# Two leading batches, a one-instruction first tile and row gathers on one queue, in the last stage of a linear-attention and spectral-mixing kernel

## The chip, the cores and the metric

The kernel runs on one NeuronCore of one Trainium2 chip. The metric is the device time of one execution in microseconds (us). Executions scatter by about 0.4 us (standard deviation).

## The reference, cut to what matters

```python
def _attn_ref(q, k, v):                      # batch 8, heads 8, sequence 576, head size 64
    q_p, k_p = phi(q), phi(k)                # phi(x) = elu(x) + 1
    kv = einsum('bhsd,bhse->bhde', k_p, v)
    return einsum('bhsd,bhde->bhse', q_p, kv) / (q_p . sum(k_p) + 1e-6)

def _moe_ref(x, w_r, w_i, w_ch):             # x: 8 x 576 x 512
    X = rfft(x, axis=1)                      # only the first 64 modes are kept
    Y = X[:, :64] times (w_r + i w_i), one 512 x 512 complex matrix per mode
    u = x + irfft(Y)
    return u + maximum(u @ w_ch, 0)
```

The weights are 2 x 64 matrices of 512 x 512 in float32, 134 MB in all. The output is 9.44 MB of float32.

## The kernel before

The output has 36 tiles of 128 rows by 512 columns, stored in 18 pairs (16 pairs of `x_main`, two of `x_tail`). A tile needs all 64 modes, so no output tile can be finished before the last mode's weights have arrived. The kernel prepares all it can ahead of that: modes 0 to 31 are folded into `x` and into `E = x @ w_ch` early; modes 32 to 55 are brought into the form `YZ[b]` (one tile for each batch: Y, and Z = Y @ w_ch) during modes 56 to 60. The last eight modes of all batches lie in one tile, `last`, and small DMAs ("gathers", 32 KB each) copy each batch's 16 rows out of it into the free rows 48 to 63 and 112 to 127 of `YZ[b]`. After that, each tile of the tail takes an identity matmul that brings in E, one for Z, a ReLU on ScalarE in place, one for Y, and an add of `x` on VectorE; a pair is then stored.

Batch 0 was a "leading" batch: modes 32 to 55 were applied to its tiles ahead of time, and in the tail it reads `last` directly, through a matrix `inv0_sb` that picks its rows, without waiting for a gather.

```python
for i, dst in enumerate((inv2_sb, inv0_sb)): ...        # row-picking matrices
...
def fold_first(t):                                      # batch 0's four tiles, in modes 56 to 60
    acc = inv2_sb[0:2*NF, rows].T @ YZ[0][0:2*NF, 0, :]  # one matmul
    x = acc + x                                         # VectorE
...
# the end, after the last mode (cut)
for h in range(2): last[:, 1, cols] = YT_rows.T @ wch   # 8 matmuls, two copies
y_ps = transposes of YT_rows                            # 4 transposes
nc.scalar.copy(out=last[:, 0, :], in_=y_ps)
for b in (1, 2, 3, 4, 5, 6, 7, 0):
    eng = nc.sync if b in (1, 2) else nc.gpsimd
    for h in range(2):
        eng.dma_start(out=YZ[b][64*h+48 : 64*h+64, :, :], in_=last[b::B, :, :])
...
rectified(0); rectified(1); channels(2); finish(0)      # rectified: matmuls of Z, then ReLU
channels(3); finish(1); rectified(2); rectified(3)      # channels: matmuls of E
finish(2)                                               # finish: matmuls of Y, add of x, store
for n in range(4, len(pairs)):
    channels(n); rectified(n); finish(n - 1)
finish(len(pairs) - 1)
```

`FILL` adds dummy matmuls in modes 61 to 63 (5, 11 and 6 of them), which keep TensorE busy.

## Time and profile before

The median is 430.0 us (three runs, 429.66 to 430.55); the profiled execution spans 428.4 us.

| part of the span | read from | value |
|---|---|---|
| weight stream, to the last mode's cast | timeline, VectorE | to 394.61 us |
| last mode to `last` complete | timeline, VectorE and ScalarE | to 396.79 us |
| first output store issued | timeline, SyncE | 399.34 us |
| VectorE's last add ends | timeline | 420.90 us |
| stores end (last 0.1 us above 100 GB/s) | windows | 425.5 us |

The last row is read from the windows view in stretches of 0.1 us (its columns are explained below; the last one is GB/s). This is the last stretch above 100 GB/s; the next has 82:

```profile
425.41:425.51 0.10, 0.00 (x0) 0.00 (x0) 0.00 (x0) 0.00 (x0) 0.00 (x0) 0.50 0.41 143
```

The page of the kernel before, part 2: two rows of the span in 40 slices of 10.7 us. The first is the busy share of the 16 DMA engines in tenths, the second what they wrote.

```profile
DMA  8999999999999999999999999999999999995697
GB/s 149 207 208 209 209 210 208 211 215 213 217 213 213 214 213 214 215 212 213 213 213 213 214 214 213 214 213 212 213 214 214 213 214 213 212 214 115 239 405 288
```

For 36 slices the DMA engines are full with the weight stream (the count is of bytes written, as bf16; the float32 bytes read are twice as many). Then comes a slice of 115 GB/s in which the stream drains and nothing can be stored yet, then a slice of 239 that ramps up, and then stores at 405 GB/s. Part 4 of the same page, the chain of work that ended last, by engine:

```profile
DMA 78%; PE 6%; DVE 6%; issue 5%; POOL 2%; ACT 1%; DVEq 0%; POOLq 0%
```

The timeline of VectorE (DVE) in the tail: start, busy time, engine, line, operation, output and inputs, and in brackets the idle time before it and who ended it.

```profile
394.61 0.23 DVE L402 CAST YT<-y_last 128x64 f16<-128x64 f32 x1 [3.11 <-PE y_last L391]
395.98 0.42 DVE L765 CAST last<-zl 128x256 f16<-128x256 f32 x1 [1.14 <-PE zl L757]
398.20 1.29 DVE L684 TENSOR_TENSOR x_main<-acc,x_main 128x512 f32<-128x512 f32 x2 [1.79 <-PE acc L610]
399.42 1.22 DVE L689 TENSOR_TENSOR x_main<-acc,x_main 128x1024 f32<-128x1024 f32 x1
401.34 4.76 DVE L689 TENSOR_TENSOR x_main<-acc,x_main 128x1024 f32<-128x1024 f32 x4 [0.69 <-PE acc L610]
406.37 1.23 DVE L689 TENSOR_TENSOR x_main<-acc,x_main 128x1024 f32<-128x1024 f32 x1 [0.27 <-PE acc L610]
...
419.62 1.28 DVE L684 TENSOR_TENSOR x_main<-acc,x_main 128x512 f32<-128x512 f32 x2
```

VectorE waits 1.79 us for the first tile, 0.69 us for pair 2 and 0.27 us for a gather; then it adds pair after pair. The Trainium skill, "VectorE: DVE Perf Modes", section "The TRN2 errata — SBUF-src ops pay a fixed extra latency per instruction", gives (N+151)/0.96 ns for a float32 tensor add of N columns; that is 691 ns for 512 and, as an estimate from the formula, 1,224 ns for 1,024. This trace agrees, with one of the two inputs in PSUM: the earlier float32 adds of 512 columns have a mean of 691 ns, the pair adds of 1,024 columns 1,223 ns.

The timeline of SyncE's queue, four gathers and then the first stores:

```profile
396.81 2.48 SPq L772 DMA_DIRECT2D YZ<-last  x4
399.34 8.62 SPq L665 DMA_DIRECT2D out_dram<-x_main  x8
```

The first tile's add ended at 398.9 us, but its store was issued only at 399.34, when SyncE had got through its gathers. Last, the windows view, in stretches of 1 us. The last two columns are the share of the 16 DMA engines in use and their GB/s; before them come the stretch's length, the engines' busy times with counts, and the granted TensorE clock.

```profile
397.61:398.61 1.00, 1.00 (x6) 0.49 (x5) 0.41 (x1) 1.00 (x3) 1.00 (x3) 1.00 0.22 66
398.61:399.61 1.00, 1.00 (x5) 0.23 (x3) 1.00 (x3) 0.34 (x1) 1.00 (x3) 1.00 0.47 135
399.61:400.61 1.00, 0.87 (x5) 0.25 (x4) 1.00 (x1) 0.81 (x2) 1.00 (x3) 1.00 0.38 109
400.61:401.61 1.00, 0.88 (x4) 0.11 (x2) 0.31 (x2) 1.00 (x3) 1.00 (x3) 1.00 0.90 305
401.61:402.61 1.00, 1.00 (x8) 0.26 (x6) 1.00 (x2) 0.65 (x2) 1.00 (x3) 1.00 0.92 291
402.61:403.61 1.00, 1.00 (x6) 0.15 (x4) 1.00 (x1) 0.98 (x3) 0.22 (x1) 1.00 1.06 410
```

If one adds up 1 minus the share (taking a share above 1 as 1), the DMA engines left 0.78 + 0.53 + 0.62 + 0.10 + 0.08 = 2.11 us unused here. In the next 1 us they are at 0.88, and from 404.6 us on at 1.00 or above until the stores end.

### The profile page before, as it was taken

What the parts mean: (1) busy time and instruction counts of PE and PEld (TensorE: products, weight loads), DVE (VectorE), ACT (ScalarE), POOL (GpSimd) and SP (SyncE); (2) the same over time, 40 slices, a digit from 0 to 9 for tenths busy, and PEclk for the clock granted to TensorE, in tenths of its full rate; (3) what the DMA queues carried; (4) which work ended last, traced back from release to release, by engine and by line L of the source; (5) the groups of instructions that cost most, each with busy time, mean ns of one, the idle gap of its engine ahead of it and who ended that gap; (6) DMA issues with size and microseconds to landing.
All of it is one profiled execution on the core that took longest, in us unless ns stands there. A gap on an engine that the chain in (4) does not pass through costs nothing.

```text
span 428.4 us, 6567 instructions
## 1 busy us (share of the span) xinstructions
PE 275.9 (64%) x2674; PEld 157.4 (37%) x2674; DVE 208.6 (49%) x426; ACT 149.2 (35%) x231; POOL 94.5 (22%) x171
## 2 busy tenths in 40 slices
PE   0358678786019665655333777787777776988991
PEld 0346556663004433333111334433434433654320
DVE  0699998956003755556100434433443344221792
ACT  3587766631102100000000244443444342220881
POOL 4233223112201321122122121221221221110500
PEclk9999865667558755555555599988999999699996
DMA  8999999999999999999999999999999999995697
GB/s 149 207 208 209 209 210 208 211 215 213 217 213 213 214 213 214 215 212 213 213 213 213 214 214 213 214 213 212 213 214 214 213 214 213 212 214 115 239 405 288
DMA packets 35917, 92.52 MB, mean 216 GB/s; under 512 B 3248, under 2 KB 16432, under 8 KB 35888
## 3 DMA queue, kind: packets, MB, share of 16 engines
q0 software_dynamic: 32192, 82.20, 98.7%
q1 hardware_dynamic: 3696, 9.91, 6.0%
q8 instruction: 21, 0.34, 0.3%
q14 instruction: 8, 0.07, 0.0%
HBM read 163.93 MB, written 9.44 MB: 405 GB/s over the span
## 4 chain that ended last, share of the span: by engine, by line
DMA 78%; PE 6%; DVE 6%; issue 5%; POOL 2%; ACT 1%; DVEq 0%; POOLq 0%
DMA wi<-in_moe_w_i_dram 61%; DMA wr<-in_moe_w_r_dram 5%; DMA pick_sb<-row_pick 4%; DMA q<-in_q_dram 4%; DMA k<-in_k_dram 4%; PE P L349 2%; DVE x L267 2%; PE acc L610 2%; PE acc L649 1%; POOL YZ L772 1%; DMA YZ<-last 1%; DVE qe L195 1%; ACT ke L182 1%; DVE q L189 1%; DVE rd L264 0%
## 5 line engine op out<-in xcount | busy, mean ns | idle before, releaser
L349 PE MATMUL P<-wi,xt_c 128*32 128x512 bf16 x252 | 36.5, 518 | 45.3 <-DMA wi<-in_moe_w_i_dram 45.3
L360 ACT CAST ys<-P 128x512 f16<-128x512 f32 x31 | 18.2, 586 | 134.5 <-PE P L349 134.5
L110 POOL DMA_DIRECT2D wr<-in_moe_w_r_dram x64 | 34.1, 532 | 125.2 <-PE P L349 100.7
L349 PEld LDWEIGHTS <-xt_c 128*32 128x32 bf16 x504 | 30.0, 153 | 83.7 <-issue 72.6
L110 POOL DMA_DIRECT2D wi<-in_moe_w_i_dram x65 | 34.6, 532 | 115.0 <-PE P L349 87.1
L358 DVE CAST ys<-P 128x512 f16<-128x512 f32 x32 | 22.1, 691 | 76.0 <-PE P L349 76.0
L349 PE MATMUL P<-wr,xt_c 128*32 128x512 bf16 x252 | 36.8, 523 | 26.1 <-DMA wr<-in_moe_w_r_dram 24.0
L535 DVE TENSOR_TENSOR x_main<-ya,x_main 128x512 f32<-128x512 f32 x32 | 22.1, 691 | 42.5 <-PE ya L531 42.5
L554 PE MATMUL eps<-wch,xTw 128*128 128x512 f16 x144 | 39.6, 401 | 0.0
L146 PEld LDWEIGHTS <-qT 64*128 64x128 f16 (+1 forms) x640 | 23.5, 125 | 39.6 <-issue 18.9
L365 PE MATMUL yt<-pick_sb,ys 128*128 128x16 f16 x252 | 16.4, 175 | 26.4 <-DMA pick_sb<-row_pick 15.8
L537 ACT CAST x16w<-x_main 128x512 f16<-128x512 f32 x32 | 19.8, 618 | 36.3 <-DVE x_main L535 36.3
L562 ACT CAST E<-eps 128x512 f16<-128x512 f32 (+1 forms) x40 | 21.3, 543 | 24.8 <-PE eps L554 24.8
L146 PE MATMUL num<-kv,qT 64*128 64x65 f16 (+1 forms) x320 | 13.4, 223 | 21.6 <-ACT kv L242 18.8
L365 PEld LDWEIGHTS <-ys 128*128 128x128 f16 x252 | 12.1, 102 | 41.3 <-issue 18.5
L182 ACT ACTIVATE qe<-q 128x1152 f16<-128x1152 f16 x16 | 17.7, 1156 | 22.1 <-DMA q<-in_q_dram 22.1
L211 PE MATMUL qTp<-id,qe 128*128 128x128 f16 x144 | 16.7, 311 | 12.5 <-DVE qe L195 12.1
L267 DVE TENSOR_TENSOR x<-num,rd 128x512 f16<-128x512 f32 x32 | 22.1, 692 | 1.1
L146 PE MATMUL nw<-kv,qT 64*128 64x65 f16 (+1 forms) x320 | 20.0, 235 | 1.4 <-DVE x_tail L506 1.0
L659 ACT ACTIVATE acc<-acc 128x512 f32<-128x512 f32 x36 | 19.1, 581 | 3.2 <-PE acc L610 0.9
L211 PEld LDWEIGHTS <-qe 128*128 128x128 f16 x144 | 14.7, 147 | 13.4 <-DVE qe L195 12.1
L182 ACT ACTIVATE ke<-k 128x1152 f16<-128x1152 f16 x16 | 17.7, 1155 | 4.9 <-DMA k<-in_k_dram 4.9
(90 smaller groups left out, 427.3 us busy)
## 6 DMA issues: line engine op xcount, KB each, us to landing
wr<-in_moe_w_r_dram POOLq DMA_DIRECT2D x64, 512.0 KB, 18.8
wi<-in_moe_w_i_dram POOLq DMA_DIRECT2D x63, 512.0 KB, 18.8
out_dram<-x_main SPq DMA_DIRECT2D x14, 512.0 KB, 4.6
q<-in_q_dram POOLq DMA_DIRECT2D x8, 576.0 KB, 13.4
k<-in_k_dram POOLq DMA_DIRECT2D x8, 576.0 KB, 14.8
v<-in_v_dram POOLq DMA_DIRECT2D x8, 576.0 KB, 16.9
out_dram<-x_main SPq DMA_DIRECT2D x4, 256.0 KB, 4.2
out_dram<-x_tail SPq DMA_DIRECT2D x2, 512.0 KB, 5.3
```

Of the source, the lines that this page charges most:

```text
L110: tc.keep_in_program_order(nc.gpsimd.dma_start(out=w[:, dcs], in_=rows_of[:, dcs, :]))
L146: mm = nc.tensor.matmul(num[hpo][orow, c0 : c0 + 65], qT[rows, hpp, h2, cols], kv_sb[rows, hpp, h2, :])
L182: pin(nc.scalar.activation(out=ev[:, c], in_=heads(nm, b)[:, c], func=AF.Exp))
L211: nc.tensor.transpose(qT_ps[:, j].rearrange("p t r -> p (t r)"), phi["q", b][:, hpp, j].rearrange("p o d -> p (o d)"), id16,)
L267: nc.vector.tensor_tensor(out=dst.rearrange("p (o c d) -> p o c d", o=2, c=4), in0=nv[:, :, :, 0:64], in1=rden.unsqueeze(3).broadcast_to([ ...
L349: nc.tensor.matmul(P[dc * 32 : dc * 32 + 32, :], xt_cols(dc, t, kk), w[:, dc, :], start=(t == 1), stop=(t == 0), tile_position=(0, dc * 32),)
L358: fixed(nc.vector.tensor_copy(out=st, in_=P))
L365: nc.tensor.matmul(yt_ps[:, ec, kk % 8, :], st[:, ec * 128 : ec * 128 + 128], pick_sb)
L535: pin(nc.vector.tensor_tensor(out=x, in0=acc, in1=x, op=ALU.add))
L537: pin(nc.scalar.copy(out=x16w[t], in_=x))
L554: nc.tensor.matmul(e_ps, xT[:, c, :], wch16[:, c, :], start=(c == 0), stop=(c == NDC - 1))
L562: pin(nc.scalar.copy(out=dst, in_=e_ps[:, cols]))
```

## The change

The intent is to start the output earlier and to take waits out of its first pairs. There are three parts.

1. Batch 1 becomes a leading batch too, and for both the Z part is prepared as well, so that pairs 0 to 3 wait for no gather in the tail: besides `last` they need only E, in which the Z part is now contained.
2. Tile 0 gets its Y part ahead, from a matmul of its own, so that one VectorE instruction does ReLU and final add; the transposes go in front of the products with `w_ch`.
3. All gathers are issued by GpSimd, and the leading batches need one instead of two: 14 gathers instead of 16.

```diff
-    inv0_sb = ystage.tile([128, S], F16, name="inv0_sb")
+    N_LEAD = 2
+    lead_sb = [ystage.tile([128, S], F16, name=f"lead{b}_sb") for b in range(N_LEAD)]
 ...
-    def fold_first(t: int):
+    def fold_lead(t: int):                 # for the tiles of both leading batches
 ...                                        # matmul of Y, add to x, as before, and then:
+        e = E0[b][:, jj * D : jj * D + D]
+        acc = bank(f"zb{t}")
+        pin(nc.tensor.matmul(acc, id16, e, start=True, stop=False))
+        pin(nc.tensor.matmul(acc, sel_rows, YZ[b][0 : 2 * NF, 1, :], start=False, stop=True))
+        pin(nc.scalar.copy(out=e, in_=acc))
 ...                                        # transposes and their copy moved ahead of the products
+    pin(nc.tensor.matmul(y0, lead_sb[0][:, rows_of(0)], last[:, 0, :]))
+    pin(nc.vector.tensor_tensor(out=x_of(0), in0=y0, in1=x_of(0), op=ALU.add))
-    for b in (1, 2, 3, 4, 5, 6, 7, 0):
-        eng = nc.sync if b in (1, 2) else nc.gpsimd
-        for h in range(2):
-            eng.dma_start(out=YZ[b][64 * h + 48 : 64 * h + 64, :, :], in_=last[b::B, :, :])
+    for b in (2, 3, 0, 1, 4, 5, 6, 7):
+        for h in range(1 if b < N_LEAD else 2):
+            nc.gpsimd.dma_start(out=YZ[b][64 * h + 48 : 64 * h + 64, :, :], in_=last[b::B, :, :])
 ...
-    rectified(0)
+    add_inverse(0, 1)
+    on_bank(0, {0}, nc.vector.scalar_tensor_tensor(
+        out=x_of(0), in0=accs[0][:, 0], scalar=0.0, in1=x_of(0), op0=ALU.max, op1=ALU.add))
+    store(0, 1)
+    relu(0, 1)
     rectified(1)
     channels(2)
-    finish(0)
+    add_inverse(0, 0, (1,))
+    on_bank(0, {1}, nc.vector.tensor_tensor(out=x_of(1), in0=accs[0][:, 1], in1=x_of(1), op=ALU.add))
+    store(1, 1)
     channels(3)
-    finish(1)
     rectified(2)
+    finish(1)
     rectified(3)
```

## The prediction

> **What bounds the kernel now.** Median 430.0 us, profiled span 428.4. Until 394.3 us it is the weight stream: the 40 slices show full DMA engines at about 213 GB/s, and the chain of waits is 78% DMA, up to the last piece of wi at 394.24. A tail of 34 us follows. In the timeline: cast of the last mode 394.61, `last` complete 396.79, first store issued 399.34, last VectorE add ended 420.9; the windows show stores at about 405 GB/s from 402.5 to 425.3. So 5 us pass from last weight to first store, then 9.44 MB leave at a rate that the DMA engines (1.29 us a pair of tiles) and VectorE (1.22 us a pair) share almost equally.
>
> **What changes in the tail.**
> - Transposes go ahead of the wch products: ScalarE copies `last[:,0]` at about 395.3 instead of 396.2; `last` is complete at about 396.65 (before 396.79).
> - Tile 0's spectral part is added by VectorE (0.69 us) at about 396.65; one VectorE instruction (estimate 0.69 us, as L684 reads the same operands) replaces ScalarE's ReLU (0.58), a matmul and the add. First store at about 398.1 instead of 399.34.
> - SyncE loses 4 gather issues (0.58 us each), which held the first store 0.5 us beyond its add. GpSimd issues 14 instead of 12 (0.49 each), until about 403.8, but the first four pairs need none, so the 0.27 us wait on VectorE at 406.1 should go. The Trainium skill, "DMA: Bandwidth & Descriptors", "Issuing engines are not separate DMA queues", says that issuing from several engines saves only sequencer time; I expect no change in the gathers' transfer.
> - Against it: pair 1's ReLUs come later and VectorE waits twice: pair 1's add at about 399.8 (before 399.42), pair 2's at 401.0 (before 401.34), back to back from there.
>
> So of 1.2 us won at the first store only 0.4 to 0.9 reaches the last one.
>
> **What moves ahead of the tail.** Modes 56 to 60 take eight ScalarE copies (0.59 each), four adds (0.69) and about 6.5 us of TensorE (8 tiles x 3 matmuls x 0.27) in place of 1.1. The weights pace this stage at 4.9 us a mode. TensorE waited there 1.76 and 1.43 us and ran at clock 0.50 from 363.9 to 370.8, after a window in which it was a quarter busy. With work in that gap I expect full clock (the skill, "TensorE: Matmul & The Clock Gate", "What's actually happening": the clock follows activity in windows of about 3.4 us), and TensorE about 3 us behind the weights at mode 60, level again by mode 62. The last weights are issued 17 us before landing, so this lag does not move 394.3.
>
> **Prediction:** 429.3 us, 428.0 to 430.8 in 8 of 10. Faster by over 2%: 0.01; within 2%: 0.97; slower by over 2%: 0.02.
>
> **Right if:** the last wi piece lands at 394.3 plus or minus 0.3 and its cast follows within 0.4 us; first store near 398.1; VectorE back to back from pair 2, ending near 420.3; stores at about 405 GB/s, ending 0.4 to 1 us earlier.
> **Wrong if:** TensorE runs at half clock in modes 56 to 60 and is still behind at mode 63 (1 to 3 us slower), or the ReLUs of pairs 1 and 2 leave longer gaps on VectorE (no gain), or the early stores fill the DMA engines sooner and 1.2 us or more is kept (428.5).

## The result, and the profile after

The first measurement gave a median of 429.3 us (four runs, 428.78 to 429.85) against 429.88 us, with a ratio of 0.9984 (95% interval 0.9967 to 1.0001). Ratios here are the mean time of one kernel's runs over that of the other's of the same rounds, so not quite the ratio of the medians quoted. The gain measured is 0.16%, and the interval includes 1, that is, no change at all. The profiled execution spans 427.4 us.

The page of the changed kernel, the same two rows, and the chain:

```profile
DMA  8999999999999999999999999999999999996698
GB/s 146 207 208 209 209 210 209 211 214 214 218 212 214 213 214 213 215 212 214 213 213 214 213 214 212 214 214 214 214 213 214 214 214 212 213 213 135 211 404 313
```

```profile
DMA 73%; PE 12%; DVE 6%; issue 5%; POOL 1%; ACT 1%; DVEq 0%; POOLq 0%
```

The weight stream is the same, and the store rate of 404 GB/s too. The chain passes more through TensorE (PE): the last weight load was issued later, at 378.9 instead of 377.3 us, since TensorE released its buffer later. It still landed for the product at 394.3. VectorE's timeline:

```profile
394.64 0.22 DVE L402 CAST YT<-y_last 128x64 f16<-128x64 f32 x1 [2.69 <-PE y_last L391]
396.22 0.42 DVE L765 CAST last<-zl 128x256 f16<-128x256 f32 x1 [1.36 <-PE zl L757]
396.57 0.68 DVE L768 TENSOR_TENSOR x_main<-y0l,x_main 128x512 f32<-128x512 f32 x1
397.36 0.69 DVE L784 SCALAR_TENSOR_TENSOR x_main<-acc,x_main 128x512 f32<-128x512 f32 x1
398.46 0.69 DVE L793 TENSOR_TENSOR x_main<-acc,x_main 128x512 f32<-128x512 f32 x1 [0.41 <-PE acc L616]
399.75 7.04 DVE L695 TENSOR_TENSOR x_main<-acc,x_main 128x1024 f32<-128x1024 f32 x6 [0.60 <-PE acc L616]
...
418.86 1.28 DVE L690 TENSOR_TENSOR x_main<-acc,x_main 128x512 f32<-128x512 f32 x2
```

The cast comes at the same time (394.64 and 394.61). The fused instruction took 0.69 us, as an add alone does. There is no wait left from pair 1 on, and the last add ends at 420.14, 0.76 us earlier than before. SyncE's first stores:

```profile
398.08 9.41 SPq L671 DMA_DIRECT2D out_dram<-x_main  x8
```

The first store is issued 1.26 us earlier. And yet the stores' end, relative to the cast, moved from 30.9 us to 30.7 only (both read to 0.1 us; this is the last stretch above 100 GB/s, the next has 82):

```profile
425.24:425.34 0.10, 0.00 (x0) 0.00 (x0) 0.00 (x0) 0.00 (x0) 0.00 (x0) 0.50 0.32 123
```

The windows from 3 to 9 us after the cast say why:

```profile
397.64:398.64 1.00, 1.00 (x6) 0.47 (x5) 0.59 (x2) 1.00 (x3) 1.00 (x3) 1.00 0.11 33
398.64:399.64 1.00, 1.00 (x6) 0.54 (x5) 0.51 (x1) 0.82 (x2) 1.00 (x4) 1.00 0.80 277
399.64:400.64 1.00, 1.00 (x6) 0.45 (x5) 0.89 (x1) 1.00 (x4) 1.00 (x3) 1.00 0.83 289
400.64:401.64 1.00, 1.00 (x7) 0.30 (x5) 1.00 (x2) 0.75 (x3) 1.00 (x3) 1.00 0.50 158
401.64:402.64 1.00, 1.00 (x8) 0.31 (x6) 1.00 (x2) 0.89 (x2) 1.00 (x3) 1.00 0.93 358
402.64:403.64 1.00, 1.00 (x8) 0.26 (x6) 1.00 (x2) 0.85 (x2) 1.00 (x3) 1.00 0.91 295
```

The early stores fill the second and third stretch (0.80 and 0.83, before 0.47 and 0.38), but the DMA engines then run dry in the fourth (0.50, before 0.90), because pair 1 comes 0.33 us later than before (single1 below, which stores half of it sooner, has 0.75 there). That the gathers from one queue drag on may add to it; this is argued and not shown. The unused time is 1.92 us instead of 2.11. The gain of 1.26 us at the first store is 0.2 us of DMA time. The kernel before has one profile only; the end at 30.7 us came again in a second profile of the changed kernel.

The two profiled spans differ by 1.0 us, but 0.8 of that lies after the last bytes (2.9 us before, 2.1 after). A second profile of the changed kernel had 2.7 us there, so this part is scatter and not the change.

### The profile page after: what moved, and what is told of

Same layout as the page of the kernel before. It is cut to its first block, busy times and chain, and to the rows that moved or that the text cites. A ratio compares the mean times of both kernels' runs of the same rounds, so it can differ in the third digit from the quotient of the medians. Undisturbed runs are those within 1.5% of the kernel's fastest.

```text
span 427.4 us, 6617 instructions
## 1 busy us (share of the span) xinstructions
PE 285.4 (67%) x2692; PEld 158.9 (37%) x2692; DVE 212.1 (50%) x432; ACT 153.7 (36%) x240; POOL 95.6 (22%) x173
## 4 chain that ended last, share of the span: by engine, by line
DMA 73%; PE 12%; DVE 6%; issue 5%; POOL 1%; ACT 1%; DVEq 0%; POOLq 0%
DMA wr<-in_moe_w_r_dram 48%; DMA wi<-in_moe_w_i_dram 13%; DMA pick_sb<-row_pick 4%; DMA q<-in_q_dram 4%; DMA k<-in_k_dram 4%; PE P L349 3%; PE acc L616 3%; DVE x L267 2%; PE acc L655 2%; PE z L579 1%; PE zb L606 1%; PE eps L557 1%; PE zb L605 1%; DVE qe L195 1%; ACT ke L182 1%
## 5 line engine op out<-in xcount | busy, mean ns | idle before, releaser
L349 PE MATMUL P<-wi,xt_c 128*32 128x512 bf16 x252 | 37.8, 536 | 39.7 <-DMA wi<-in_moe_w_i_dram 39.7
L349 PEld LDWEIGHTS <-xt_c 128*32 128x32 bf16 x504 | 28.9, 155 | 76.3 <-issue 65.2
L557 PE MATMUL eps<-wch,xTw 128*128 128x512 f16 x144 | 41.3, 415 | 0.0
L665 ACT ACTIVATE acc<-acc 128x512 f32<-128x512 f32 x34 | 18.1, 581 | 2.3 <-PE acc L616 1.7
```

Source lines behind the costliest of these rows:

```text
L349: nc.tensor.matmul(P[dc * 32 : dc * 32 + 32, :], xt_cols(dc, t, kk), w[:, dc, :], start=(t == 1), stop=(t == 0), tile_position=(0, dc * 32),)
L557: nc.tensor.matmul(e_ps, xT[:, c, :], wch16[:, c, :], start=(c == 0), stop=(c == NDC - 1))
```

## The experiments

Two theories of what sets the end of the tail run through them. Theory S: the 16 DMA engines do; the tail ends when the stores and gathers have passed, plus the time that the engines stood unused before they were full. Rival V: VectorE's adds do. Theory A says that the earlier first store is what gains. All kernels below are the changed kernel with one edit.

### The changed kernel again (r_after)

No edit; five runs.

> The changed kernel again, with more rounds, since its first interval (0.9967 to 1.0001) does not tell the change from no change. If the 0.6 us between the two medians (429.88 and 429.30) is real, the ratio is 0.9975 to 0.9993 with an upper end below 1. If it was scatter, the ratio lies within 0.0008 of 1 and the interval holds 1.

Measured: 429.68 us median against 429.86, ratio 0.9992 (0.9979 to 1.0006). The ratio lies in both of the ranges expected, but the interval includes 1. All nine runs of the changed kernel (two calls) have a mean of 429.49 us, the 31 runs of the kernel before (four calls) 429.99 us, with standard deviations of 0.47 and 0.36. The difference of 0.50 us has a standard error of 0.17 (the root of 0.47²/9 + 0.36²/31), if one neglects that the calls ran on several chips. A gain of a few tenths of a microsecond is likely, and no more can be said. The profiles show 0.2 us of it; whether the rest is real, and where it would come from, stays open.

### The first four gathers back on SyncE (u_gather)

```diff
-            nc.gpsimd.dma_start(out=YZ[b][64 * h + 48 : 64 * h + 64, :, :], in_=last[b::B, :, :])
+            eng = nc.sync if b in (2, 3) else nc.gpsimd
+            eng.dma_start(out=YZ[b][64 * h + 48 : 64 * h + 64, :, :], in_=last[b::B, :, :])
```

> The changed kernel with the first four row gathers (batches 2 and 3) issued by SyncE as before. Theory A (the gain comes from the earlier start of the output stream): SyncE is held for four issues of 0.58 us from about 396.8 us, so the first store is issued near 399.2 us instead of 398.08, and the time rises by 0.3 to 0.8 us, that is, most of the gain goes. Rival B (the queue does not matter, because VectorE and the stream of adds set the end): below 0.2 us.

Measured: 429.52 us median, ratio 0.9985 (0.9971 to 0.9998). SyncE's timeline shows the expected delay of the first store, by 1.16 us relative to the cast:

```profile
396.81 2.47 SPq L772 DMA_DIRECT2D YZ<-last  x4
399.33 7.97 SPq L671 DMA_DIRECT2D out_dram<-x_main  x8
```

It cost nothing: the mean time is 0.1 us below the changed kernel's, and the stores' end came 30.5 us after the cast. Theory A falls. With two queues issuing, the last gather is issued at 402.1 us instead of 403.9, so gathers instead of stores use the early DMA time, and the unused time is 1.88 us, as good as 1.92:

```profile
397.73:398.73 1.00, 1.00 (x6) 0.48 (x5) 0.58 (x2) 1.00 (x3) 1.00 (x3) 1.00 0.28 78
398.73:399.73 1.00, 1.00 (x7) 0.53 (x5) 0.52 (x1) 0.82 (x2) 1.00 (x4) 1.00 0.41 119
399.73:400.73 1.00, 1.00 (x6) 0.45 (x5) 0.88 (x1) 1.00 (x4) 1.00 (x4) 1.00 0.53 172
400.73:401.73 1.00, 1.00 (x7) 0.29 (x5) 1.00 (x2) 0.75 (x3) 1.00 (x3) 1.00 0.97 318
401.73:402.73 1.00, 1.00 (x8) 0.31 (x6) 1.00 (x2) 0.90 (x2) 0.38 (x1) 1.00 0.95 316
402.73:403.73 1.00, 1.00 (x8) 0.26 (x6) 1.00 (x2) 0.85 (x2) 0.00 (x0) 1.00 0.98 363
```

The Trainium skill, "DMA: Bandwidth & Descriptors", section "Issuing engines are not separate DMA queues", says that issuing on several engines only saves the sequencers' time. This run agrees: the split moved issue times by more than 1 us and the end by 0.2 us, to the earlier side.

### One leading batch (u_lead)

```diff
-    N_LEAD = 2
+    N_LEAD = 1
-    for b in (2, 3, 0, 1, 4, 5, 6, 7):
+    for b in (1, 2, 3, 0, 4, 5, 6, 7):
```

> The changed kernel with one leading batch instead of two, as before; all gathers stay on GpSimd, batch 1's first. Theory A: pair 2 needs gathers that land at about 400.2 us and its ReLUs wait for them; VectorE then waits 0.7 to 1.3 us before pair 2, and the time rises by 0.3 to 1.0 us. Rival B (the second leading batch buys nothing, as its gathers were in time before): within 0.2 us. In both, TensorE has about 2.2 us less work in modes 57 and 58 and is level with the weights earlier.

Measured: 430.14 us median, ratio 1.0001 (0.9986 to 1.0015); by the means, 0.5 us slower than the changed kernel (430.00 and 429.49), with a standard error of 0.3, so not shown by the times alone. The wait is there, but ahead of pair 1 and not of pair 2: in this program pair 2's matmuls of Z stand in front of pair 1's of Y, and the trace shows TensorE waiting for a gather there (0.22 us at 398.64), before it goes on with pair 1. VectorE's lines:

```profile
398.03 0.69 DVE L793 TENSOR_TENSOR x_main<-acc,x_main 128x512 f32<-128x512 f32 x1 [0.41 <-PE acc L616]
400.08 6.88 DVE L695 TENSOR_TENSOR x_main<-acc,x_main 128x1024 f32<-128x1024 f32 x6 [1.36 <-PE acc L616]
```

The wait is 1.36 us instead of 0.60, the DMA engines' unused time 2.52 us, and the stores end 31.4 us after the cast, the latest of all. So the second leading batch is worth about 0.7 us in this order of the work, by the profiles. Without it the other parts of the change gain nothing: the end at 31.4 us is later than the 30.9 of the kernel before. Whether another order of the matmuls would do as well was not tried.

### Tile 0 as before (u_fuse)

```diff
-    (matmul y0, add of y0 to tile 0; fused ReLU and add; store; ReLU of tile 1; ...)
+    rectified(0)
     rectified(1)
     channels(2)
+    finish(0)        # two single tiles, ReLU on ScalarE
```

> The changed kernel with tile 0 handled as before (ScalarE ReLU, a matmul, an add on VectorE). Theory A: the first store is issued near 398.9 us instead of 398.08, and pair 1's add comes up to 0.4 us earlier, so the two cancel in part: 0 to 0.4 us slower. Rival C (the fused tile is what won the time): 0.6 us slower or more.

Measured: 429.53 us median, ratio 0.9990 (0.9976 to 1.0005), so within the scatter of the changed kernel; rival C falls. In its profile the first store is issued 4.53 us after the cast (changed kernel: 3.44), which is later than expected, pair 1 comes 5.35 us after it (expected up to 0.4 us earlier than 5.11, in fact later), and the stores end 31.0 us after it. The profile says 0.3 us slower; the times don't show it.

### Fewer bytes to store (half_stores)

```diff
-        store(t0, 2)
+        store(t0, 1 if n >= 4 else 2)
```

> Wrong on purpose: from pair 4 on, eleven stores write one tile instead of two, 2.9 MB less, with all compute as it was. Theory S (the stores' bandwidth sets the end; VectorE finishes early and stores queue up): the time falls by 1.5 to 2.4 us, to the last add at about 420.1 us plus a store's smallest landing time of 2.5 us. Rival V (VectorE's adds set the end): the time falls by less than 0.5 us.

Measured: 426.59 us median, ratio 0.9921 (0.9907 to 0.9934), in the mean 2.9 us below the changed kernel, more than the 1.5 to 2.4 expected. Output wrong, as intended. The stores end 28.1 us after the cast, 2.6 us after VectorE's last add, which is again 25.50 us after the cast. Rival V falls: with VectorE's work unchanged, the end came 2.6 us sooner. The DMA engines are no longer full in this run (0.46 to 0.83 in the stretches of 1 us from 411 to 420 us), so that now VectorE's last add and the store after it set the end, and the gain is less than the bytes left out.

### No gathers (no_gather)

```diff
-    for b in (2, 3, 0, 1, 4, 5, 6, 7):
-        for h in range(1 if b < N_LEAD else 2):
-            nc.gpsimd.dma_start(...)
```

> Wrong on purpose: no row gathers at all (0.46 MB, 4.4% of the 16 DMA engines' time in the last 36 us, that is 1.6 us). Theory S: these 1.6 us are taken from the stores, and the time falls by 0.6 to 1.6 us. Rival V: less than 0.3 us, as VectorE has no wait on a gather left.

Measured: 428.37 us median, ratio 0.9962 (0.9949 to 0.9976), 1.15 us below the changed kernel in the mean. The result passes the tolerance, but it lacks the last eight modes of six batches and of the tails of all, so it is no valid version. Theory S holds: 0.46 MB of gathers cost 1.1 us of the tail, though VectorE does not wait for them (its last add ends 25.47 us after the cast, with 25.50 in the changed kernel). The profile says how: the stores end 29.6 us after the cast, and the unused time from 3 to 9 us rises to 2.81 us. End minus unused is 26.8 us instead of 28.8, so by this sum the gathers took 2.0 us of DMA time, of which 0.9 lay in time that is otherwise unused.

### A little more VectorE work (slow_dve)

```diff
+        if n >= 4:
+            pin(nc.vector.tensor_copy(out=actwarm, in_=actwarm))     # 128 x 1
```

> VectorE gets one copy of a single column[...] after each of thirteen adds from pair 4 on, in all 0.8 to 1.3 us. Theory S: VectorE ends that much later, but the time rises by 0.4 us at most, because stores are waiting for the DMA engines anyway. Rival V: the time rises by 0.8 to 1.3 us.

Measured: 429.76 us median, ratio 0.9999 (0.9984 to 1.0014). It decided nothing: the thirteen copies of 0.14 us each overlap with the adds, and VectorE's last add ended 25.56 us after the cast, with 25.50 in the changed kernel.

### More VectorE work (slow_dve2)

```diff
+        if n >= 4:
+            pin(nc.vector.tensor_tensor(out=inv_sb[:, 0:192], in0=inv_sb[:, 192:384],
+                                        in1=inv_sb[:, 384:576], op=ALU.max))
```

> The one-column copies of the earlier run overlapped with the adds and cost VectorE nothing, so that run decided nothing. Now each of thirteen adds is followed by a maximum over 192 f16 columns[...], so that VectorE's last add ends about 1.3 to 2.6 us later relative to the last mode's cast (25.5 us after it in the changed kernel). Theory S (the DMA engines set the end; about 2 us of stores are waiting when VectorE stops): the stores' end moves by at most half of that. Rival V (VectorE sets it): by all of it.

Measured: 429.38 us median, ratio 0.9988 (0.9973 to 1.0003). VectorE's timeline:

```profile
408.15 1.22 DVE L695 TENSOR_TENSOR x_main<-acc,x_main 128x1024 f32<-128x1024 f32 x1
409.29 0.25 DVE L697 TENSOR_TENSOR inv_sb<-inv_sb 128x192 f16<-128x192 f16 x1
409.45 1.22 DVE L695 TENSOR_TENSOR x_main<-acc,x_main 128x1024 f32<-128x1024 f32 x1
...
419.85 1.28 DVE L690 TENSOR_TENSOR x_main<-acc,x_main 128x512 f32<-128x512 f32 x2
```

An add now starts every 1.30 us, and the last one ends at 421.13, that is 26.69 us after the cast (394.44) instead of 25.50, just short of the range expected. The stores' end stays at 30.7 us after it. VectorE has 1.2 us to give, and rival V falls a second time.

### More TensorE work in mode 61 (pe_extra)

```diff
-    FILL = {61: (2, 2, 1), 62: (5, 3, 3), 63: (6,)}
+    FILL = {61: (6, 6, 1), 62: (5, 3, 3), 63: (6,)}
```

> Eight filler matmuls more in mode 61 (0.27 us each, 2.2 us). In the changed kernel TensorE does not wait for weights from 366.7 us until mode 63, and its two waits there are 0.39 us each. If that is all the slack (theory T), the cast of the last mode and with it the whole tail move by 1.0 to 1.6 us. The prediction's claim in its wide form (a lag of TensorE does not move 394.3, as the last weights are issued 17 us before they land): less than 0.3 us.

Measured: 429.37 us median, ratio 0.9985 (0.9972 to 0.9999), and a cast at 393.89 us in the profile. Theory T falls for this run: eight more matmuls in front of the end, in its profile 1.7 us (two groups of 1.46 us instead of 0.59), cost nothing. Its profile had TensorE at full clock throughout modes 56 to 60, which the changed kernel's first profile had not, so the slack read from that one was the slack of a slow execution. The second profile of the changed kernel, at full clock too, shows more slack: TensorE waits 0.56 and 0.81 us for mode 62's weights and 0.34 and 0.63 us for mode 63's. What the edit costs in an execution at half clock is not shown.

### Two tries at a better version (single1 and best)

In single1 pair 1 is added and stored as two single tiles.

```diff
-        single = n == len(pairs) - 1
+        single = n in (1, len(pairs) - 1)
-        add_inverse(n, 0)
+        if not single:
+            add_inverse(n, 0)
         for i, t in enumerate(pairs[n]):
             if single:
+                add_inverse(n, 0, (i,))
```

> A try at a better version: pair 1 is added and stored as two single tiles, so that VectorE's 0.6 us of waiting before pair 1 is used and the third tile's store goes out near 399.9 us instead of 401.0. Theory S: the gap in the output stream between 398 and 402 us closes in part, 0.2 to 0.5 us faster than the changed kernel. Rival V: at most 0.2 us, as pair 2 still waits for its ReLUs until 400.8 us.

Measured: 429.76 us median, ratio 0.9994 (0.9981 to 1.0006). The gain expected of 0.2 to 0.5 us is not seen: the mean is 0.2 us above the changed kernel's, within the scatter. In the profile the unused time fell to 1.74 us and the stores' end by 0.1 us. In best, SyncE also issues batch 2's two gathers, in the time before the first store.

```diff
+            eng = nc.sync if b == 2 else nc.gpsimd
-            nc.gpsimd.dma_start(...)
+            eng.dma_start(...)
```

> A try at a better version: pair 1 as two single tiles, and SyncE, which is idle from 396.7 to 398.1 us, issues batch 2's two gathers in that time (2 x 0.58 us), so that GpSimd is done 1 us earlier and the first store is not held. Theory S counts the DMA engines' unused time in the six us from 3 us after the cast on: 1.9 us in the changed kernel, 1.6 expected here, so 0.2 to 0.5 us faster than the changed kernel, which may be lost in the scatter of about 0.4 us.

Measured: 429.74 us median, ratio 0.9991 (0.9979 to 1.0004). In its profile the unused time is down to 1.59 us and the stores end 30.4 us after the cast, 0.3 us sooner than in the changed kernel, as theory S says. The times don't show it (mean 0.1 us above the changed kernel's). No version here beats the changed kernel beyond the scatter.

### All profiles in one table

Each row is one profiled execution. Times are in us after the last mode's cast, except the cast itself. "Unused" is the sum of 1 minus the DMA share from 3 to 9 us after the cast, in stretches of 1 us; "end" is the end of the last 0.1 us with over 100 GB/s.

| kernel | cast at | first store | last add ends | unused | end | end minus unused |
|---|---|---|---|---|---|---|
| before | 394.61 | 4.73 | 26.29 | 2.11 | 30.9 | 28.8 |
| changed | 394.64 | 3.44 | 25.50 | 1.92 | 30.7 | 28.8 |
| r_after | 395.12 | 3.44 | 25.51 | 1.94 | 30.7 | 28.8 |
| u_gather | 394.73 | 4.60 | 25.50 | 1.88 | 30.5 | 28.6 |
| u_lead | 394.20 | 3.44 | 26.02 | 2.52 | 31.4 | 28.9 |
| u_fuse | 394.95 | 4.53 | 25.73 | 2.19 | 31.0 | 28.8 |
| slow_dve2 | 394.44 | 3.43 | 26.69 | 1.95 | 30.7 | 28.8 |
| pe_extra | 393.89 | 3.45 | 25.51 | 1.95 | 30.8 | 28.9 |
| single1 | 394.56 | 3.44 | 25.50 | 1.74 | 30.6 | 28.9 |
| best | 394.96 | 3.45 | 25.51 | 1.59 | 30.4 | 28.8 |

(half_stores, no_gather and slow_dve are left out: the first two move fewer bytes, and the third changed nothing.) The last column is constant within 0.3 us, while the first store moves by 1.3 us and the last add by 1.2 us without the end following them. That is theory S in one table. In part it is bookkeeping: with nearly the same bytes to move, the column has to be constant as long as the DMA engines stay full from 9 us after the cast to the end. That they do is what the traces add: in all ten, each 1 us from there to 29 us after the cast has a share of 0.87 or more, most of 1.00 or more. The second column explains part of the scatter of the times: the cast alone, which hangs on the last piece of the weight stream, moves by 1.2 us from one execution to another. The stretch from the stores' end to the end of the span moves by another 0.8 us (2.1 to 2.9). Each is more than the change brings.

## Why the prediction was right

- **The time.** Predicted 429.3 us (428.0 to 430.8), measured 429.3 us; the pooled gain is about 0.5 us. That the median agrees to 0.1 us is in part luck: the repeat of the same kernel gave 429.68 us, and the range also held 430.0 us, that is, no change.
- **The start of the tail.** `last` complete at 396.65 (measured 396.64), first store near 398.1 (398.08), pair 1 near 399.8 (399.75), back to back from pair 2 (from pair 1, measured), last add near 420.3 (420.14). These came from adding up durations in the old trace along the new order on each engine. The wait of 0.27 us for a gather went, as predicted.
- **What bounds the tail.** Here a step was off. The prediction had the DMA engines and VectorE "share almost equally", and carried "0.4 to 0.9" of the first store's 1.2 us to the end. VectorE has 1.2 us to spare (slow_dve2), and what reaches the end is only the drop in unused DMA time: VectorE's last add did end 0.76 us earlier, but the stores' end moved by 0.2 us in the profile, and 0.4 to 1 us had been predicted. The step that failed is thus the overlap: time gained on VectorE was taken as time gained by the stores. It also listed SyncE's gathers, "which held the first store", as a cost; u_gather shows that holding it costs nothing as long as the gathers use the DMA engines meanwhile.
- **Gathers.** The prediction expected no change from the queue, and u_gather bears that out. It did not see that the gathers themselves cost 1.1 us at the end (no_gather).
- **TensorE in modes 56 to 60.** "I expect full clock" failed in the profiled execution. The windows view of the changed kernel's first profile and then of its second, with the granted clock as the third figure from the end:

```profile
368.00:370.00 2.00, 2.00 (x9) 0.45 (x9) 0.69 (x1) 0.75 (x2) 0.53 (x1) 0.71 1.03 207
370.00:372.00 2.00, 2.00 (x5) 0.30 (x4) 1.05 (x2) 0.81 (x2) 0.00 (x0) 0.50 1.09 219
```

```profile
368.00:370.00 2.00, 2.00 (x14) 0.80 (x13) 1.10 (x2) 0.58 (x1) 0.53 (x1) 1.00 1.04 209
370.00:372.00 2.00, 2.00 (x11) 0.62 (x9) 1.53 (x3) 1.38 (x3) 0.00 (x0) 1.00 1.08 217
```

The clock is 0.71 and 0.50 in one and 1.00 in the other, from the same program, so the windows of about 3.4 us that the prediction took from the skill did not foretell the first of these executions (see the list at the end). In the first, TensorE was level with the weights at mode 63 and not at mode 62. The conclusion still held: the last mode's cast did not move, and pe_extra put 1.7 us more in front of it for nothing, though at full clock.

## What to carry to other kernels

Where the end of a kernel is a drain through the DMA engines, count the time in which those engines stand unused from the moment that they could work, and judge each edit by that sum: an earlier first transfer is worth only as much as it lowers it, and it is worth little if the second transfer then comes late. Small transfers that nobody waits for still cost their DMA time in such a drain. And when the expected gain is smaller than the scatter of an upstream event (here the landing of the last weights), measure from that event in the profile, because the total time can't decide.

## What the Trainium skill lacked or had wrong

- "TensorE: Matmul & The Clock Gate", section "What's actually happening", ties the half clock to a window of about 3.4 us without activity. In the changed kernel's first profile the clock was at 0.50 from about 368.9 to 375.7 us although TensorE's longest wait in the ten microseconds before was 0.52 us; a second profile of the same program had waits of 0.77 and 0.52 us in that stage and 1.00 throughout. The matmuls bear the record out: a group of eight took 1.98 us in the spell and 1.14 us after it. The page's section "A second HAM failure mode: psum-queue depth-cycling" does tell of a kernel whose clock went back and forth with short idle times between groups of matmuls, without their length. What starts such a spell here stays open.
- "DMA: Bandwidth & Descriptors", section "Where 436 GB/s comes from", says that the HBM limit of about 358 GB/s per core binds transfers between HBM and SBUF. For this kernel, which runs on one core, it did not: stores from SBUF ran at 405 GB/s for 20 us. The same page's table of loads says so for a single core, too (425 GB/s at 16 MB); what it lacks is a figure for stores.
- The same page has no one cost of issuing a copy: its breakdown of the fixed 2 us has about 50 ns for the sequencer and calls the making of descriptors small, while a comparison made for a later chip gives 512 sequencer cycles a copy for the chips before it. A gather of 32 KB took 0.58 us of SyncE's queue and 0.49 us of GpSimd's. Nor has it the cost of copies from SBUF to SBUF of 16 rows beside a full stream: 14 of them, 0.46 MB, took 2.0 us of the DMA engines' time and moved the end by 1.1 us.
- "VectorE: DVE Perf Modes", section "The DRAIN you can't avoid", says that the next operation starts when the pipe is empty, and that one that is not held starts earlier. It has no figure for how much earlier. Here thirteen copies of one column, 0.14 us each, between adds moved the last add by 0.06 us in all.
- That page's timing formula is for `tensor_tensor` and has no term for `scalar_tensor_tensor`; with one PSUM and one SBUF input of 512 float32 columns it took 0.69 us, as the plain add does.
